# An HGRN2 attention and PReLU network kernel on one core: f, q and v loaded one step further ahead

## The chip, the cores and the metric

The kernel runs on one core of one Trainium2 chip. The metric is the device time of one execution in microseconds (us); smaller is better. A time is the median of the runs shown. One execution is also recorded by the hardware profiler, and its trace is what the text reads.

## The reference

Two blocks stand one behind the other. The first is a gated linear recurrence for 4 batches, 8 heads, 768 positions and a head dimension of 48; the second is a two-layer network with 3072 rows, 384 inputs and 2048 hidden units.

```python
f = 1.0 / (1.0 + np.exp(-f_logit))
state = np.zeros((B, H, D, D)); y = np.zeros_like(q)
for t in range(S):
    state = f[:, :, t, :, None] * state + np.einsum('bhd,bhe->bhde', k[:, :, t], v[:, :, t])
    y[:, :, t] = np.einsum('bhd,bhde->bhe', q[:, :, t], state)

x = y.transpose(0, 2, 1, 3).reshape(B * S, H * D)        # 3072 x 384
h = x @ w_in                                              # 384 x 2048
g = np.maximum(h, 0.0) + alpha * np.minimum(h, 0.0)
out = g @ w_out                                           # 2048 x 384
```

## The kernel before

The work is cut into twelve steps. A step takes 128 positions of two batches; the steps alternate between the two pairs of batches (`bp` 0 and 1), so that steps n and n+2 belong to the same pair. For each step three parts are defined: `preparation` (the gates' running products, on VectorE, ScalarE and GpSimd), `attention` (the scores, the output products and the state) and `network` (the two layers, the second one with seven products per 2x2 blocks instead of eight, named A to E).

Nothing schedules this on its own. Each part stores its pieces of work under short words, and one list, `ORDER`, names word and step in the order in which they are issued; each engine runs its share of that list strictly in turn. `ORDER` is made by `flat` from two tables: `FIRST`, written out word for word for the opening, and `USUAL`, which is repeated for n = 4 to 12. In `USUAL` a word without a mark belongs to step n, `-` to step n-1, `+` to step n+1. So one block n issues attention of step n, most of the network of step n-1 and the preparation of step n+1. A word whose step is 12 or more is dropped.

The words that matter here:

- `ld` loads a step's inputs in five DMAs: `ld.0` is f, `ld.1` is q, `ld.2` is k (512 KB each, L343), `ld.3` and `ld.4` are the two halves of v (192 KB each, L348). For steps above 4 they are issued by SyncE (SP). In `USUAL` they stand in the first line, behind the score products `r0`, `x0`, `r1`, `x1` of step n, and load step n+1.
- f, q and k have one buffer each (`mine`, one buffer per tag). f is read last in a preparation by `le` (a product on VectorE, L235 `ut<-ut,f`), q by `qc` (a copy on ScalarE, L354). k is read by the score products `r0` and `r1` of its own step, and thus by the next block; its load has to wait for them.
- v lies in `vs`, one tile for each pair of batches, which also holds the state in other rows. v of step n is read by the state products `pd` (L655) and the output products `y0`, `y1` (L730) of block n.
- `mv` (L767) moves the attention's output `y` into the network's input `xT` with ten small DMAs, four issued by SP, four by ScalarE, two by GpSimd. The first layer of that step, `n0` to `n7` (L799), reads it in the next block.
- `km` (L492) moves the transposed keys `kt` into `ksn` with sixteen small DMAs, all from SP. `ksn` shares its buffer with `y`, so the first of them waits until all of `xT` has landed. `pd` of the next block reads `ksn`.
- `d1` and `e` end with the two stores of a step's output (L845), also from SP.

Each DMA issued by SP or ScalarE takes the next of eight completion counters in turn, and is issued only once the DMA that had that counter before, eight such DMAs earlier, has landed.

```python
def loads():
    return {"A": nc.scalar, "G": nc.gpsimd, "V": nc.sync}.get(letter[0], nc.gpsimd if 0 < n <= FROM else nc.sync)
...
several(w, "ld" + mark, [lambda a=a: load(*a) for a in (("f", fT), ("q", qT), ("k", kT))]
        + [lambda cc=cc: load_v(cc) for cc in range(NC2)])
```

Of the kernel before, what the change touches and what calls it, by code (L numbers as in the profile page):

```python
# [67 lines left out]
"""  # L68

USUAL = """  # L70
r0 R0 x0 X0 n0- g0- G0- n1- g1- G1- r1 R1 x1 X1 n2- g2- G2- n3- g3- G3- S0- pd of oc0 oc1 m0 n4- g4- G4- ld+ sg+ kr+ qc+ l1+ l2+ l3+ c0+ c1+ c2+
c3+ n5- g5- G5- n6- g6- G6- n7- g7- G7- S1- sc+ A1- B- ka- le+ k4+ e2+ p00A p01A p02A p03A p10A p11A p12A p13A y0 y1 C1- D- u2- ke+ kt+ e3+ e4+ sa+
e5+ m1 z0A z1A mv A2- C2- d0- oa- e6+ km+ e7+ sb+ fs+ E- u3- b- d1- s00+ s01+ s10+ s11+ e-
"""

STEPS = 12
FROM = 4


def flat(first, usual):  # L80
    out = []
    for token in first.split():
        word, step = token.split(":")
        out.append((word, int(step)))
    for n in range(FROM, STEPS + 1):
        for token in usual.split():
            step = n + {"+": 1, "-": -1}.get(token[-1], 0)
            if step < STEPS:
                out.append((token.rstrip("+-"), step))
    return out  # L90


ORDER = flat(FIRST, USUAL)


# [935 lines left out]
```

## Time and profile before

| | before |
|---|---|
| median of 3 runs | 607.54 us (607.3 to 616.0) |
| profiled execution | 607.44 us, span 605.6 us |
| TensorE (PE) busy | 585.1 us, 97% of the span |
| VectorE (DVE) busy | 489.6 us, 81% |
| ScalarE (ACT) busy | 242.4 us, 40% |
| GpSimd (POOL) busy | 102.9 us, 17% |
| mean DMA rate | 83 GB/s, 50.41 MB |

The page gives each engine's busy time and its share of the span; a table of 40 slices shows where in the span it falls, and the chain of waits follows the work that ended last back through what released it. The "timeline" lists instructions with their start, their duration and, in brackets, the idle time before them. For a DMA the time shown is that of its issue on the engine's queue (SPq is SP's, ACTq is ScalarE's); when its data has landed is told separately, as the time from issue to landing. The span is 1.84 us shorter than the profiled execution's own time.

In the usual blocks the steps repeat every 47 us. The xT moves of steps 4 to 11 are issued at 222, 269, 316, 363, 411, 458, 505 and 552 us of the span.

### The profile page before, as it was taken

The page shows a single profiled execution, that of the slowest core. Times are in us where ns is not written, and L with a number is a line of the kernel's source. Part 1 is how long each engine was busy: PE and PEld are TensorE (multiplying, and loading weights), DVE is VectorE, ACT ScalarE, POOL GpSimd, SP SyncE. Part 2 cuts the span into 40 slices and gives each one's busy share as a digit, 9 for nine tenths or more (in the row PEclk, how much of TensorE's full clock was granted, in tenths as well). Part 3 has the DMA queues.
Part 4 walks back from the last instruction along what each step waited for, and adds up shares of the span by engine and source line. Part 5 has one row for each costly group of instructions (what it writes and reads, how often), then busy time and mean ns, then how long its engine had stood idle before and what let it go on. Part 6 is the DMA issues. An engine that isn't in the chain of part 4 may idle for free.

```text
span 605.6 us, 18807 instructions
## 1 busy us (share of the span) xinstructions
PE 585.1 (97%) x8042; PEld 527.7 (87%) x8042; DVE 489.6 (81%) x990; ACT 242.4 (40%) x464; POOL 102.9 (17%) x142
## 2 busy tenths in 40 slices
PE   3799999999999999999999999999999999999998
PEld 2699767898998899899899899799899899889997
DVE  8898999896868889889889899889899889761251
ACT  5688824433311542452452361271261362223110
POOL 6538562654230000000000000000000000000000
PEclk9999999999999999999999999999999999999999
DMA  8786272222112513402502502502602601201000
GB/s 286 241 298 225 72 258 52 65 59 45 49 35 29 162 27 58 130 22 37 155 11 42 160 3 50 162 0 45 169 0 42 166 8 39 44 2 28 27 0 27
DMA packets 73955, 50.41 MB, mean 83 GB/s; under 512 B 47264, under 2 KB 63264, under 8 KB 73872
## 3 DMA queue, kind: packets, MB, share of 16 engines
q1 hardware_dynamic: 65616, 39.07, 23.8%
q10 hardware_dynamic: 7216, 8.30, 4.7%
q0 software_dynamic: 1040, 1.84, 1.2%
q8 instruction: 64, 1.05, 0.7%
q14 instruction: 19, 0.16, 0.1%
HBM read 36.21 MB, written 4.72 MB: 68 GB/s over the span
## 4 chain that ended last, share of the span: by engine, by line
PE 92%; DMA 3%; DVE 2%; ACT 1%; issue 1%; SPq 0%; DVEq 0%
PE ph L799 37%; PE pa L894 10%; PE pc L894 9%; PE pd L894 5%; PE pb L894 5%; PE pe L894 5%; PE py L730 4%; PE ph L817 4%; PE qu L537 3%; PE raw L517 3%; PE po L859 3%; DMA w_in_raw<-in_w_in 2%; PE state L655 2%; PE off L617 1%; DMA k<-in_kT 1%
## 5 line engine op out<-in xcount | busy, mean ns | idle before, releaser
L799 PE MATMUL ph<-xT,w_in_sb 128*128 128x256 f32 x1056 | 237.2, 382 | 0.9 <-DVE gate L809 0.6
L799 PEld LDWEIGHTS ph<-xT,w_in_sb 128*128 128x128 f32 x1056 | 198.0, 190 | 30.9 <-issue 1.7
L809 DVE SCALAR_TENSOR_TENSOR gate<-neg,om,ph 128x256 f32<-128x256 f32 x176 | 76.3, 476 | 48.8 <-ACT neg L805 48.5
L805 ACT ACTIVATE neg<-ph 128x512 f32<-128x512 f32 x88 | 51.7, 598 | 156.5 <-PE ph L799 134.6
L767 POOL DMA_DIRECT2D xT<-y x22 | 12.0, 549 | 373.6 <-ACT y L739 371.2
L894 PE MATMUL pa<-w_out_sb,gate 128*128 128x192 f32 x352 | 61.9, 328 | 0.0
L894 PE MATMUL pc<-t,S 128*128 128x192 f32 x352 | 61.6, 328 | 0.0
L894 PEld LDWEIGHTS pa<-w_out_sb,gate 128*128 128x128 f32 x352 | 57.8, 190 | 1.9 <-DVE gate L809 1.0
L894 PEld LDWEIGHTS pc<-t,S 128*128 128x128 f32 x352 | 57.4, 190 | 0.6
L544 DVE COPY_PREDICATED ad<-mquad,qu 128x160 f32<-128x160 int32 (+6 forms) x140 | 41.5, 299 | 5.5
L524 DVE COPY_PREDICATED ad<-mraw,raw 128x256 f32<-128x256 int32 (+2 forms) x96 | 41.1, 444 | 4.7 <-ACT ad L582 2.0
L235 DVE TENSOR_TENSOR ut<-ut,fs 128x128 f32<-128x128 f32 (+7 forms) x62 | 41.0, 663 | 0.8
L453 ACT COPY A<-q 48x512 f32<-48x512 f32 x40 | 24.7, 617 | 38.4 <-DVE q L235 38.0
L368 ACT COPY ut<-qd 128x256 f32<-128x256 f32 (+1 forms) x52 | 32.0, 633 | 12.1 <-DVE qd L235 10.0
L920 ACT ACTIVATE o<-pa 128x192 f32<-128x192 f32 x11 | 3.6, 331 | 69.1 <-PE pa L894 65.4
L898 DVE SCALAR_TENSOR_TENSOR Csum<-pc,Csum 128x192 f32<-128x192 f32 x22 | 7.9, 358 | 28.6 <-PE pc L894 28.3
L894 PE MATMUL pd<-w_out_sb,S 128*128 128x192 f32 x176 | 30.5, 326 | 0.2 <-DVE gate L809 0.2
L894 PE MATMUL pb<-t,gate 128*128 128x192 f32 x176 | 30.5, 327 | 0.0
L716 ACT COPY A<-ad 32x256 f32<-32x256 f32 x74 | 29.6, 400 | 2.1 <-DVE ad L544 0.7
L894 PE MATMUL pe<-w_out_sb,S 128*128 128x192 f32 x176 | 30.4, 326 | 0.0
L894 PEld LDWEIGHTS pd<-w_out_sb,S 128*128 128x128 f32 x176 | 28.8, 190 | 0.4 <-ACT neg L805 0.4
L894 PEld LDWEIGHTS pb<-t,gate 128*128 128x128 f32 x176 | 28.9, 190 | 0.1
(137 smaller groups left out, 837.0 us busy)
## 6 DMA issues: line engine op xcount, KB each, us to landing
w_in_raw<-in_w_in SPq DMA_DIRECT2D x7, 767.2 KB, 7.7
f<-in_fT SPq DMA_DIRECT2D x10, 512.0 KB, 4.2
q<-in_qT SPq DMA_DIRECT2D x10, 512.0 KB, 5.1
out<-o SPq DMA_DIRECT2D x23, 192.0 KB, 2.1
w_out_raw<-in_w_out SPq DMA_DIRECT2D x5, 767.8 KB, 7.3
k<-in_kT SPq DMA_DIRECT2D x7, 512.0 KB, 7.2
vs<-in_v SPq DMA_DIRECT2D x16, 192.0 KB, 7.2
ksn<-kt SPq DMA_DIRECT2D x80, 32.0 KB, 2.0
```

Source lines behind the costliest of these rows:

```text
L235: (nc.gpsimd if beside[0] else nc.vector).tensor_tensor(*a)
L368: w[f"c{r}{mark}"] = lambda r=r: nc.scalar.copy(q4()[:, gs, :, r], qdv[r][:, gs, :, 0])
L453: copy(A[halves(cc)[1], u0:u1, par * HP:(par + 1) * HP, CH * cc:CH * (cc + 1)], x["q3"][rows(par)].rearrange("p (u h c) s t -> p u h c (s ...
L524: nc.vector.copy_predicated(adu[:, :, :, d:4], mraw[:, d, :, d:4].bitcast(I32).unsqueeze(1).broadcast_to((128, H, NB, n_)), rv[:, :, QO[d] ...
L544: nc.vector.copy_predicated(ad[:, u, :, :, 4 * m:DB], mquad[:, lo:lo + n_].bitcast(I32).unsqueeze(1).unsqueeze(1).broadcast_to((128, 2, HP ...
L716: copy(A[s_, u, :, s_], ad[s_, u].rearrange("p r h t -> p (r h) t"))
L730: nc.tensor.matmul(to[64 * par:64 * par + 64, u, o:o + CH], lhsT=vs[bp][:, cc, u, hd * D:hd * D + 64], rhs=A[:, u, par * HP + hp, CH * cc: ...
L799: nc.tensor.matmul(ph[f][:, j * T:(j + 1) * T], lhsT=w_in_sb[:, kt, m * 128:(m + 1) * 128], rhs=x["T"][:, kt], start=(kt == 0 and j == 0), ...
L805: nc.scalar.activation(neg[f], ph[f].rearrange("p (j t) -> p j t", j=2), AF.Relu, scale=-1.0)
L809: nc.vector.scalar_tensor_tensor(gate[:, m % NH, m // NH], neg[f][:, j], om[:, m:m + 1], ph[f].rearrange("p (j t) -> p j t", j=2)[:, j], A ...
L817: nc.tensor.matmul(ph[u, g][:, j * C:(j + 1) * C], lhsT=w_in_sb[:, kt, m * 128:(m + 1) * 128], rhs=x["T"][:, kt, u * C:(u + 1) * C], start ...
L894: nc.tensor.matmul(p[name][:, 0:DH], lhsT=of(f), rhs=by(f), start=(f == 0 and not more), stop=(f == NH - 1), skip_group_check=True)
```

## The change

Only the order is changed, in the table `USUAL` and in `flat`, which reads it. `ld+` becomes `ld.2+`: of step n+1 only k is loaded at the old place. The loads of f, q and both halves of v go behind `mv`, with a second `+`: they belong to step n+2. For n = 4 the loads of step 5 that no earlier block has issued are put ahead of k at the old place. No instruction is added or taken away.

```diff
-... m0 n4- g4- G4- ld+ sg+ kr+ qc+ l1+ l2+ l3+ c0+ c1+ c2+
+... m0 n4- g4- G4- ld.2+ sg+ kr+ qc+ l1+ l2+ l3+ c0+ c1+ c2+
-e5+ m1 z0A z1A mv A2- C2- d0- oa- e6+ km+ e7+ sb+ fs+ E- u3- b- d1- s00+ s01+ s10+ s11+ e-
+e5+ m1 z0A z1A mv ld.0++ ld.1++ ld.3++ ld.4++ A2- C2- d0- oa- e6+ km+ e7+ sb+ fs+ E- u3- b- d1- s00+ s01+ s10+ s11+ e-
@@ def flat
-            step = n + {"+": 1, "-": -1}.get(token[-1], 0)
+            step = n + token.count("+") - token.count("-")
+            if token == "ld.2+" and n == FROM:
+                out += [(word.rstrip("+"), step) for word in usual.split() if word.endswith("++")]
```

The order moves on SP alone; the other four engines issue the same instructions in the same order. In the middle of the program SP issues before, from the xT moves of step 7 (`xT_3_4380`) on, with the loads of step 9 (`f_4_4742` and what follows) at the end of the stretch:

```order
98 L767 DMACopy xT_3_4380<-y_3_4377 48x2x128
99 L767 DMACopy xT_3_4380<-y_3_4377 16x2x128
100 L767 DMACopy xT_3_4380<-y_3_4377 48x2x128 x2
101 L492 DMACopy ksn_4_4411<-kt_4_4367 32x8x32 x4
102 L492 DMACopy ksn_4_4411<-kt_4_4367 32x8x16 x4
103 L492 DMACopy ksn_4_4411<-kt_4_4367 32x8x32 x4
104 L492 DMACopy ksn_4_4411<-kt_4_4367 32x8x16 x4
105 L845 DMACopy out<-o_0_3_4446 128x384
106 L845 DMACopy out<-o_0_3_4407 128x384
107 L343 DMACopy f_4_4742<-in_fT 128x2x512
108 L343 DMACopy q_4_4744<-in_qT 128x2x512
109 L343 DMACopy k_4_4746<-in_kT 128x2x512
```

The same stretch of SP's order in the changed kernel (its lines of code stand two lower, and the numbers at the ends of the names are counters):

```order
98 L769 DMACopy xT_3_4380<-y_3_4377 48x2x128
99 L769 DMACopy xT_3_4380<-y_3_4377 16x2x128
100 L769 DMACopy xT_3_4380<-y_3_4377 48x2x128 x2
101 L345 DMACopy f_4_4391<-in_fT 128x2x512
102 L345 DMACopy q_4_4393<-in_qT 128x2x512
103 L350 DMACopy vs_76<-in_v 64x2x384 x2
104 L494 DMACopy ksn_4_4417<-kt_4_4367 32x8x32 x4
105 L494 DMACopy ksn_4_4417<-kt_4_4367 32x8x16 x4
106 L494 DMACopy ksn_4_4417<-kt_4_4367 32x8x32 x4
107 L494 DMACopy ksn_4_4417<-kt_4_4367 32x8x16 x4
108 L847 DMACopy out<-o_0_3_4452 128x384
109 L847 DMACopy out<-o_0_3_4413 128x384
```

f, q and v of step 9 now stand ahead of the sixteen ksn moves and the two stores instead of behind them; the ksn moves have four large loads between themselves and the xT moves. This happens in six blocks, n = 4 to 9.

At the first block of the usual table (n = 4) the five loads of step 5 keep their place, but k goes from the third to the last of them. SP's order there, before:

```order
55 L343 DMACopy f_2_2638<-in_fT 128x2x512
56 L343 DMACopy q_2_2640<-in_qT 128x2x512
57 L343 DMACopy k_2_2642<-in_kT 128x2x512
58 L348 DMACopy vs_76<-in_v 64x2x384 x2
59 L767 DMACopy xT_2_2802<-y_2_2799 48x2x128
60 L767 DMACopy xT_2_2802<-y_2_2799 16x2x128
61 L767 DMACopy xT_2_2802<-y_2_2799 48x2x128 x2
62 L492 DMACopy ksn_2_2833<-kt_2_2789 32x8x32 x4
```

And SP's order at that place in the changed kernel:

```order
55 L345 DMACopy f_2_2638<-in_fT 128x2x512
56 L345 DMACopy q_2_2640<-in_qT 128x2x512
57 L350 DMACopy vs_76<-in_v 64x2x384 x2
58 L345 DMACopy k_2_2644<-in_kT 128x2x512
59 L769 DMACopy xT_2_2802<-y_2_2799 48x2x128
60 L769 DMACopy xT_2_2802<-y_2_2799 16x2x128
61 L769 DMACopy xT_2_2802<-y_2_2799 48x2x128 x2
62 L345 DMACopy f_3_2813<-in_fT 128x2x512
63 L345 DMACopy q_3_2815<-in_qT 128x2x512
64 L350 DMACopy vs_75<-in_v 64x2x384 x2
```

Here v overtakes k, and the first of the six moved groups, f, q and v of step 6, follows the xT moves of step 4.

More of the change, by code (lines that the diff above doesn't have):

```diff
@@ L70 @@
 USUAL = """
-r0 R0 x0 X0 n0- g0- G0- n1- g1- G1- r1 R1 x1 X1 n2- g2- G2- n3- g3- G3- S0- pd of oc0 oc1 m0 n4- g4- G4- ld+ sg+ kr+ qc+ l1+ l2+ l3+ c0+ c1+ c2+
+r0 R0 x0 X0 n0- g0- G0- n1- g1- G1- r1 R1 x1 X1 n2- g2- G2- n3- g3- G3- S0- pd of oc0 oc1 m0 n4- g4- G4- ld.2+ sg+ kr+ qc+ l1+ l2+ l3+ c0+ c1+ c2+
 c3+ n5- g5- G5- n6- g6- G6- n7- g7- G7- S1- sc+ A1- B- ka- le+ k4+ e2+ p00A p01A p02A p03A p10A p11A p12A p13A y0 y1 C1- D- u2- ke+ kt+ e3+ e4+ sa+
-e5+ m1 z0A z1A mv A2- C2- d0- oa- e6+ km+ e7+ sb+ fs+ E- u3- b- d1- s00+ s01+ s10+ s11+ e-
+e5+ m1 z0A z1A mv ld.0++ ld.1++ ld.3++ ld.4++ A2- C2- d0- oa- e6+ km+ e7+ sb+ fs+ E- u3- b- d1- s00+ s01+ s10+ s11+ e-
 """
```

## The prediction

> **What bounds the kernel now.** I read the page first, then PE's waits from 187 us of the span on, where the usual blocks begin, then busy time by stretch, and last the timeline of one block. The page names the bound: PE.
>
> ```profile
> span 605.6 us, 18807 instructions
> PE 585.1 (97%) x8042; PEld 527.7 (87%) x8042; DVE 489.6 (81%) x990; ACT 242.4 (40%) x464; POOL 102.9 (17%) x142
> PE 92%; DMA 3%; DVE 2%; ACT 1%; issue 1%; SPq 0%; DVEq 0%
> ```
>
> 97% is an average over the span; what counts is the part that the change touches. PE's waits after 187 us are a single row, and the stretches show where it lies (columns: window, its length, then PE busy, weight loads, DVE, ACT, POOL, granted clock, DMA share, GB/s):
>
> ```profile
> PE off L617 <- issue: 0.9, 1, 0.9
> 0.00:187.00 187.00, 170.44 (x2586) 149.07 (x2586) 161.92 (x314) 97.31 (x185) 94.22 (x126) 1.00 0.45 137
> 187.00:223.00 36.00, 36.00 (x591) 31.88 (x590) 30.87 (x64) 15.50 (x30) 0.62 (x2) 1.00 0.32 79
> 364.00:412.00 48.00, 47.07 (x658) 42.81 (x657) 41.71 (x85) 18.37 (x35) 0.98 (x3) 1.00 0.27 67
> 412.00:459.00 47.00, 47.00 (x658) 42.82 (x658) 41.59 (x86) 18.43 (x35) 1.20 (x3) 1.00 0.28 69
> ```
>
> PE is busy 36.00 us of 36 and 47.00 of 47; only the stretch from 364 has a gap, 48.00 - 47.07 = 0.93 us, and its releaser is "issue", which means no engine and no load. Of PE's idle 605.6 - 585.1 = 20.5 us, 187 - 170.44 = 16.6 us lie in the opening, which the change leaves alone, and the last 3 us behind PE's last product. So a move of loads can gain 0.9 us at most as long as PE's own work stays, and can cost whatever it makes PE wait.
>
> **Who needs what, and when.** One block as the timeline has it, from the output products of step 9 on (start, duration, engine):
>
> ```profile
> 454.57 2.15 PE L730 MATMUL py<-A,vs 128*64 128x64 f32 x64
> 455.68 1.20 DVE L235 TENSOR_TENSOR ut<-ut,f 128x1024 f32<-128x1024 f32 x1
> 457.87 3.14 SPq L767 DMA_DIRECT2D xT<-y  x4
> 457.87 2.56 ACTq L767 DMA_DIRECT2D xT<-y  x4
> 461.83 1.25 DVE L485 STREAM_TRANSPOSE kt<-ks 128x1024 f32<-128x1024 f32 x1
> 463.15 11.99 SPq L492 DMA_DIRECT2D ksn<-kt  x16
> 471.53 5.45 PE L799 MATMUL ph<-xT,w_in_sb 128*128 128x256 f32 x24
> 475.25 1.01 SPq L845 DMA_DIRECT2D out<-o  x2
> 476.31 0.44 SPq L343 DMA_DIRECT2D f<-in_fT  x1
> 476.80 0.49 SPq L343 DMA_DIRECT2D q<-in_qT  x1
> 476.91 0.92 PE L517 MATMUL raw<-qd,k 48*32 48x80 f32 x64
> 477.86 0.37 SPq L343 DMA_DIRECT2D k<-in_kT  x1
> 478.27 1.32 SPq L348 DMA_DIRECT2D vs<-in_v  x2
> 483.98 0.94 PE L655 MATMUL state<-vs,ksn 64*48 64x48 f32 x64
> 489.10 1.06 ACT L352 ACTIVATE f<-f 128x1024 f32<-128x1024 f32 x1
> 503.65 1.22 DVE L235 TENSOR_TENSOR k<-k,kr 128x1024 f32<-128x1024 f32 x1
> ```
>
> The DMA part of the page has the sizes and the median time from issue to landing over all blocks:
>
> ```profile
> f<-in_fT SPq DMA_DIRECT2D x10, 512.0 KB, 4.2
> q<-in_qT SPq DMA_DIRECT2D x10, 512.0 KB, 5.1
> k<-in_kT SPq DMA_DIRECT2D x7, 512.0 KB, 7.2
> vs<-in_v SPq DMA_DIRECT2D x16, 192.0 KB, 7.2
> xT<-y SPq DMA_DIRECT2D x33, 48.0 KB, 2.2
> ```
>
> **Part 1, the wait that goes: none.** f lands at 476.31 + 4.2 = 480.5 us and is read first at 489.10: 8.6 us early. q lands at 481.9 and is read behind f; v is read no earlier than the output products, a block after those at 454.57; k lands at 485.1 and is read at 503.65. Nothing waits for these loads today, so loading them earlier is worth 0 us.
>
> **Part 2, can they start there?** f's buffer is free when the product at 455.68 ends, 456.9 us; v's when the output products end, 456.7. SP's four xT issues end at 461.0. So no load waits for its buffer (the nearest margin is 461.0 - 456.9 = 4.1 us), and nothing behind them on SP is held up by that. They take SP 0.44 + 0.49 + 1.32 = 2.25 us, until 463.3. The first ksn move was issued at 463.15, because kt ends at 461.83 + 1.25 = 463.1. On SP itself the loads thus fit into a pause: 0.1 us late.
>
> **Part 3, what is queued behind them: the sixteen ksn moves, two stores, k.** The first four moves use counters of older DMAs; moves five to eight wait for f, q and the two halves of v to land, by the turn of the counters; the last eight wait for the first eight. When does v land? In the block shown v's landing times are
>
> ```profile
> DMA to landing us min/median/max: 7.9/8.0/8.1
> ```
>
> so its second half, issued at about 479.0, lands at 487.0, and five loads of 3 x 512 + 2 x 192 = 1920 KB take 487.0 - 476.31 = 10.7 us. f, q and v are 1408 KB: 10.7 x 1408 / 1920 = 7.8 us, from 461.0 to 468.8. Upper bound: the whole 10.7 us, 471.7. The eighth ksn move then goes at about 468.8, and eight more at 11.99 / 16 = 0.75 us each end at 474.8. Before, the sixteen ended at 463.15 + 11.99 = 475.1. I take 475.5, since the moves were partly waiting for each other anyway. The landing times of ksn in that block:
>
> ```profile
> DMA to landing us min/median/max: 1.9/2.0/3.8
> ```
>
> The last one lands at 477.5 (479.3 with the longest), and the state products read ksn at 483.98. **Cover: 4.7 to 6.5 us** per block. Cost 0; were the cover gone, PE would stand still for the difference in each of six blocks.
>
> As the k row shows beside f's (7.2 against 4.2 us, with f and q queued ahead of it), a DMA lands later behind others of its queue. [...]
>
> The xT moves stand ahead of the loads on SP, and ScalarE's are issued by 457.87 + 2.56 = 460.4. With 2.2 us they land by 463.2; the first layer reads xT at 471.53, 8.3 us later. Cost 0.
>
> The two stores follow at 475.5 + and end within half a us of before. k waits for the score products that end at 476.91 + 0.92 = 477.8 in both kernels, then has the DMA engines to itself. In block 4 alone k goes behind v; with 18 us to spare (503.65 - 485.1) this is 0.
>
> **Part 4, the one gap.** How the loads lie beside PE's work changes (columns as above, in the block shown):
>
> ```profile
> 461.00:470.00 9.00, 9.00 (x71) 8.78 (x78) 8.79 (x16) 0.37 (x2) 0.00 (x0) 1.00 0.25 37
> 476.30:482.00 5.70, 5.70 (x148) 4.79 (x147) 4.30 (x12) 1.05 (x2) 0.00 (x0) 1.00 0.96 296
> ```
>
> During the loads the DMA engines are 96% busy, and PE goes through 148 matmuls in 5.7 us; where f, q and v will lie it goes through 71 in 9 us, and the DMA engines are 25% busy. The gap of 0.93 us came while loads were under way (SP and PE, two blocks earlier; the last row is from the page's list of DMA queues: packets, MB, share):
>
> ```profile
> 380.59 0.44 SPq L343 DMA_DIRECT2D f<-in_fT  x1
> 383.41 1.33 SPq L348 DMA_DIRECT2D vs<-in_v  x2
> 389.98 0.74 PE L617 MATMUL off<-q,kh 48*32 48x32 f32 x62
> 391.65 0.24 PE L617 MATMUL off<-q,kh 48*32 48x32 f32 x2 [0.93 <-issue]
> q8 instruction: 64, 1.05, 0.7%
> ```
>
> PE stopped inside a row of like products, waiting for no engine; I read it as instructions that had not arrived, since the list has a DMA queue that moves instructions and the DMA engines were taken. That happened in one of seven such windows. Bounds: -0.93 us if this goes with the loads' place, 0 if it is chance, +0.93 if a new one comes. I take -0.5, the middle between gone and kept, because the busiest mixture of loads and short products goes. [...]
>
> **The sum.** The profiled execution took 607.44 us (span 605.6 and 1.84 around it), 0.1 below the median of 607.54. 607.44 + 0 (waits) + 0 (queue) - 0.5 = **606.9 us**.
>
> **The rivals.**
>
> *Moves behind the loads (slower).* All sixteen ksn moves are held until the last load has landed, with xT drawn in by sharing DMA engines. At the upper bound that is 471.7; sixteen moves then end at 483.7 and land at 485.7 to 487.5, so that the state products stand still 1.7 to 3.5 us, six times: 10 to 21 us, 617.6 to 628.4. It decides from the point where ksn lands over 6.5 us later than I have it. For it: the k row, and a DMA share of 0.96 under loads. Against it: v alone at 468.8 and only four of the sixteen tied to loads; even all sixteen behind 468.8 would end at 480.8 and land at 482.8, still 1.2 us in time. Chance 0.07; between the two ends it crosses 2% (619.7), so 0.04 of it is beyond.
>
> *The gap goes wholly, and nothing else.* 607.44 - 0.93 = 606.5. It is inside my range; chance 0.35, beside 0.53 for the forecast itself with the gap half certain or kept (606.9 to 607.5).
>
> *The loads do not get ahead.* If a buffer were free later than I read it, say f's only after SP has reached its load, all of ksn would shift by that wait. It needs more than 4.1 us of delay to begin and 4.7 more to reach PE; what it gives short of that is 607.4 again. Chance 0.02.
>
> *A new wait elsewhere* (more gaps of the 0.93 kind, one in each of the six blocks, in the score products that run while k is loaded): 607.44 + 5.6 = 613.0. Chance 0.03; against it stands that k alone is 512 of the 1920 KB.
>
> **How the numbers follow.** Faster by over 2% would be below 595.4, and the blocks hold 0.93 us of idle PE: 0.01 for what I don't see. Slower by over 2% needs the first rival's upper part: 0.04. Within 2%, which is about what a measurement of this kernel can tell from no change: 0.95. The range: 606.5 with some 0.5 for the runs' scatter below, hence 605.9; above, two gaps of the 0.93 kind on top of 607.5 give 609.4. That leaves out the first rival, the last one and the tails, less than 2 in 10.
>
> **What would show it.** In the changed profile the loads of f, q and v stand at about 461 us of this block (SP's queue), the sixteen ksn moves still end near 475 to 476, and no row "PE state L655 <- DMA ksn" or "PE ph L799 <- DMA xT" appears among PE's waits. Each usual block stays at 47.0 us. ksn's longest landing time rises from 3.8 to about 6 us, as its first moves stand behind v. I am wrong if the state products wait for ksn, if SP shows a wait of the f load on DVE, or if PE's "issue" gaps after 187 us grow beyond 2 us.

## The result and the profile after

| | before | after |
|---|---|---|
| median of 22 runs each, in turn on one chip | 610.22 us (607.0 to 616.0) | 607.21 us (605.54 to 609.36) |
| ratio, 95% interval | | 0.9956 [0.9938, 0.9974] |
| profiled execution, span | 607.44 us, 605.6 | 608.01 us, 606.2 |

The changed kernel is faster by 0.44%, by the ratio 2.7 us of 610 with an interval of 1.6 to 3.8 (the medians lie 3.0 us apart). That lies within 2%, at 607.21 us where 606.9 was forecast; but the forecast gain was 0.5 us. The two profiled executions even stand the other way round, so the gain has to be read from the stretches and not from the spans. The head of the page after, with the chain:

```profile
span 606.2 us, 18821 instructions
PE 585.0 (97%) x8042; PEld 527.6 (87%) x8042; DVE 489.8 (81%) x990; ACT 242.1 (40%) x464; POOL 102.4 (17%) x142
PE 81%; DVE 2%; ACT 1%; issue 1%; DVEq 0%
```

PE is the bound as before. Busy time by stretch, with the columns of the prediction:

```profile
0.00:187.00 187.00, 168.77 (x2575) 147.48 (x2576) 160.50 (x311) 97.01 (x185) 93.79 (x126) 0.97 0.45 137
364.00:411.00 47.00, 47.00 (x658) 42.82 (x658) 41.72 (x86) 18.53 (x36) 1.07 (x2) 1.00 0.28 69
462.00:470.00 8.00, 8.00 (x51) 8.00 (x50) 7.82 (x14) 0.33 (x1) 0.00 (x0) 1.00 0.86 217
476.00:482.00 6.00, 6.00 (x149) 5.06 (x148) 4.62 (x13) 0.60 (x1) 0.00 (x0) 1.00 0.49 155
```

The opening, which both kernels share, was slower in this execution (168.77 us of PE work in 187, against 170.44). The stretch from 364 us, where the one gap was, is full: 47.00 of 47.00. PE has no wait left after 187 us, neither for an engine nor for "issue". The DMA engines are now 86% busy at 462 to 470 us, beside 51 long matmuls, and 49% at 476 to 482, beside 149 short ones. SP's queue and the state products of the same block:

```profile
458.52 3.10 SPq L769 DMA_DIRECT2D xT<-y  x4
461.73 0.57 SPq L345 DMA_DIRECT2D f<-in_fT  x1
462.91 1.39 SPq L350 DMA_DIRECT2D vs<-in_v  x2
464.53 12.25 SPq L494 DMA_DIRECT2D ksn<-kt  x16
478.52 0.39 SPq L345 DMA_DIRECT2D k<-in_kT  x1
484.63 0.94 PE L657 MATMUL state<-vs,ksn 64*48 64x48 f32 x64
```

The ksn moves end at 476.8 us, 18.3 us behind the start of the xT moves (before: 475.14 - 457.87 = 17.3): 1.0 us later, with the state products still 7.9 us away.

### The profile page after: what moved, and what is told of

It reads as the page before. It is cut to its first block, busy times and chain, and to the rows that moved or that the text cites. A ratio compares the mean times of both kernels' runs of the same rounds, so it can differ in the third digit from the quotient of the medians.

```text
span 606.2 us, 18821 instructions
## 1 busy us (share of the span) xinstructions
PE 585.0 (97%) x8042; PEld 527.6 (87%) x8042; DVE 489.8 (81%) x990; ACT 242.1 (40%) x464; POOL 102.4 (17%) x142
## 4 chain that ended last, share of the span: by engine, by line
PE 81%; DVE 2%; ACT 1%; issue 1%; DVEq 0%
PE ph L801 37%; PE pa L896 10%; PE pc L896 9%; PE pd L896 5%; PE pb L896 5%; PE pe L896 5%; PE py L732 3%; PE qu L539 3%; PE raw L519 2%; PE state L657 1%; PE off L619 1%; DVE ad L546 1%; DVE w_out_sb L237 0%; ACT A L455 0%; DVE gate L811 0%
## 5 line engine op out<-in xcount | busy, mean ns | idle before, releaser
L519 PE MATMUL raw<-qd,k 48*32 48x80 f32 x1536 | 22.6, 243 | 6.8 <-DVE qd L237 6.8
```

The lines of the kernel that those rows point to most:

```text
L519: nc.tensor.matmul(to[DB * j:DB * (j + 1), par, hp * C:hp * C + QW], lhsT=x["k"][r_, g * DB:(g + 1) * DB], rhs=qd[r_, g], start=True, stop ...
```

## The experiments

There are three theories. A *gap* is a time in which PE stands still and the profile names nothing that it waited for ("issue"); the *burst* is the loads of f, q, k and v that go out together, 1920 KB in the kernel before. **Collision**: the instructions of PE come late while a burst of loads is under way beside short products, and the change takes most of the burst away from there. **Lead**: f, q or v is sometimes late in executions that were not profiled. **Opening**: the gain lies outside the usual blocks or is scatter.

For every profile I read two things: the gaps of PE after 187 us, and how long the seven usual blocks take, from SP's first xT move of step 4 to that of step 11. All of them together, in the order in which they are explained below:

```
profile                              xT(4)    xT(11)   blocks   gaps of PE, us
before                               222.11   551.65   329.54   0.93
before, 2nd                          223.08   553.82   330.74   1.05  0.90
before, 3rd                          221.23   551.07   329.84   1.21
before, 4th                          221.97   554.21   332.24   1.88
before, 5th                          222.33   557.86   335.53   1.76  1.82
after                                224.01   552.30   328.29   none
after, 2nd                           221.02   549.34   328.32   none
after, 3rd                           223.36   551.46   328.10   none
no f, q, v                           223.81   552.19   328.38   none
after, two loads added behind k      221.14   553.14   332.00   1.89
f, q, v behind the ksn moves         222.32   552.55   330.23   0.95  0.24
before, 28 small matmuls added       223.39   553.69   330.30   1.72
after, 28 small matmuls added        226.83   555.15   328.32   none
before, two loads added              222.22   556.50   334.28   3.68
```

**The kernel before, against itself.**

> The kernel before, unchanged, against itself. Every theory: ratio 1.000 within the interval. What the second profile tells: the theory of collision (PE's instructions come late while the burst of loads is under way beside short products) expects one to five gaps of about 0.9 us after 187 us of the span, released by issue, all inside the 11 us behind a load of f; the theory of lead (f, q or v sometimes lands too late in the unprofiled slow executions) expects waits of ACT or PE on a DMA of f, q or vs there; the theory of the opening (the gain lies before the usual blocks, or is scatter) expects the usual blocks free of gaps and the opening to vary by 2 us or more.

Ratio 0.9974 [0.9945, 1.0004]: a comparison can be off by a quarter of a per cent. The gaps in its timeline (start, duration, engine, and in brackets the idle time ahead):

```profile
392.54 0.24 PE L617 MATMUL off<-q,kh 48*32 48x32 f32 x2 [1.05 <-issue]
440.45 0.45 PE L617 MATMUL off<-q,kh 48*32 48x32 f32 x29 [0.90 <-issue]
```

The first stands at the very instruction at which the first profile had its only gap: behind 62 of the 64 products of off. A gap by chance would hardly come back there. The second is one block later, 29 products before the end. Counted in the trace, PE's instructions behind the two gaps are number 11457 and 12737 (from 0 on, weight loads included): five times 256 apart. No wait on a DMA of f, q or vs was seen.

**No loads of f, q and v.** From step 6 on they are left out, and the steps compute on what the buffers hold; k is loaded as before.

```diff
+            if token == "ld+" and step > FROM + 1:
+                token = "ld.5+"                       # only k; f and q keep the tiles of step 5
```

> Leaves out the loads of f, q and v of steps 6 to 11 (they compute on what is there), k and all else as before. The theory of collision: 1408 of 1920 KB are gone from the burst, so the gaps go and the time comes to that of the changed kernel, ratio 0.993 to 0.997, no issue gap after 187 us. The theory of lead: nothing can be late any more, the same ratio. The theory of the opening: ratio 1.000, as the opening is the same.

0.9964 [0.9945, 0.9983], no gap, 328.38 us for the blocks: without the burst of f, q and v the gaps are gone. This takes away lateness too, so it does not part collision from lead.

**The burst put back, the lead kept.** The changed kernel with two loads into `kt` and `k4`, which are dead at that point.

```diff
-... G4- ld.2+ sg+ ...
+... G4- ld.2+ xl sg+ ...        # xl: kt <- fT, k4 <- qT, 512 KB each, on SP
```

> The changed kernel, with two loads of 512 KB added behind k in the blocks 4 to 10, into buffers that nobody reads before they are written anew: f, q and v keep their lead, but the burst beside the short products is 1536 KB again (before: 1920). The theory of collision: gaps released by issue come back, about 0.9 us each, one or more in the profile, and the ratio goes back to 0.998 to 1.005. The theory of lead: f, q and v are as early as in the changed kernel, ratio 0.993 to 0.997. The theory of the opening: 0.996 or 1.000, no gap in the usual blocks.

0.9990 [0.9965, 1.0016], and one gap, at the same instruction, 11457:

```profile
391.35 0.25 PE L626 MATMUL off<-q,kh 48*32 48x32 f32 x2 [1.89 <-issue]
```

f, q and v were as early as in the changed kernel, and the blocks take 332.00 us again. The lead theory does not explain this; the collision theory does.

**f, q and v behind the ksn moves**, at nearly the old time.

```diff
-... mv ld.0++ ld.1++ ld.3++ ld.4++ A2- C2- d0- oa- e6+ km+ e7+ ...
+... mv A2- C2- d0- oa- e6+ km+ ld.0++ ld.1++ ld.3++ ld.4++ e7+ ...
```

> The changed kernel with f, q and v of step n+2 behind the sixteen ksn moves instead of ahead of them: they go about 1 us earlier than in the kernel before (ahead of the two stores), beside the same short products. The theory of collision: as before, ratio 0.998 to 1.002, issue gaps in the profile. The theory of lead: 1 us of lead out of 8.6 is nothing, also 1.000. The theory of the opening, if it is k's new place behind v at step 5: 0.996, since that is kept here.

0.9982 [0.9962, 1.0002]; its interval holds 1.000 and comes near the changed kernel's 0.9956, so the time alone decides nothing. The profile does: a gap of 0.95 us at instruction 11457 again, and a small one of 0.24 us in front of 7361, sixteen times 256 earlier. Both stand there with k's new place behind v kept, which the opening theory had as a possible cause of the gain.

**The changed kernel again.**

> The changed kernel once more. The theory of collision: no gap released by issue after 187 us in a second profile, and a ratio of 0.995 to 0.999 (one to two gaps of 0.9 to 1.0 us gone, 1 to 2 us of 608, with the scatter of the opening on top). The theory of scatter (the first ratio of 0.9956 was mostly the opening's luck, as the unchanged kernel got 0.9974 against itself): 0.998 to 1.002.

0.9972 [0.9953, 0.9992], no gap. The gain is there a second time, smaller: 1.7 us of 608.5. The ratio alone would not prove it, since the kernel before against itself gave 0.9974.

**The boundaries moved.** 28 small matmuls in the opening, before and after the change; their results are overwritten.

```diff
-... c0b:0 iq.24:0 zm:0 ...
+... c0b:0 iq.24:0 ig:0 zm:0 ...          # ig: 28 matmuls of 128x128 by 128x32
```

> The kernel before with 28 small matmuls (56 PE instructions) added where PE idles in the opening; their results are overwritten. In the two profiles of the kernel before, all gaps released by issue after 187 us stand at places 256 PE instructions apart by a whole number (PE instruction 11457 and 12737, both 193 over a multiple of 256). The theory of collision with the fetch of instructions: the boundaries come 56 instructions earlier in the program, so that one falls into block 7, behind 62 of the 64 pairs of off, at about 345 us, and a gap of 0.9 to 2 us appears there, which no profile had; the one of the next block falls into the middle of off (behind about 34 pairs), where a smaller gap may stand, and none stands behind 62 pairs any more. Any theory in which the place in the program counts, and not the count of instructions: the gap stays behind 62 pairs of off of block 8, at about 392 us. The time: ratio 0.999 to 1.003.

> The changed kernel with the same 28 small matmuls. The theory of collision: no gap behind the instruction boundaries anywhere after 187 us, wherever they fall, since only k's 512 KB lie beside the short products; the ratio as the changed kernel's, 0.995 to 0.999. A theory by which the changed kernel was only lucky with the place of its boundaries: a gap of 0.9 us in block 7 or 8, ratio 0.998 to 1.002.

The kernel before: 1.0028 [1.0005, 1.0051], with its only gap at another place of the program:

```profile
299.81 0.25 PE L617 MATMUL off<-q,kh 48*32 48x32 f32 x4 [1.72 <-issue]
```

The gap behind off of the old block, 392 us, is gone; a new one stands two blocks earlier, in front of instruction 8897, which is again 193 over a multiple of 256. My expectation had named the block between (345 us), since I had counted 56 added instructions. The trace shows each of these matmuls as two products with two weight loads (x8098 matmuls on the page, 8042 before), so 112 were added, and in the kernel before the boundary (8897) stands 108 instructions behind the 62nd product of off in just that block at 297 us. So 112 more instructions put the boundary four instructions, or two products, ahead of that place, and the gap stands four products before the end instead of two. The count decides where the gap is, not the place in the program.

The changed kernel with the same shift has no gap at any boundary after 187 us (one of 1.27 us ends at 152.48 us, in the opening, in front of instruction 4801, also 193 over a multiple of 256) and 328.32 us for the blocks. Its ratio, 1.0005 [0.9985, 1.0025], missed what I expected. Its profile has a longer opening (226.83 us until xT of step 4, against 221 to 224 in the others), which may be the reason; that is not shown. Against the shifted kernel before it is 607.9 / 609.72 = 0.997, without an interval.

**A larger burst.**

```diff
-... G4- ld+ sg+ ...
+... G4- ld+ xl sg+ ...
```

> The kernel before with two more loads of 512 KB behind its five (into buffers that nobody reads before they are written anew): 2944 KB in one burst beside the short products, which lasts until about 491 us instead of 487 of the block shown. The theory of collision: more and longer gaps than the 0.9 and 1.9 us in all of the two profiles of the kernel before: 2 to 6 us, at the same instruction boundaries, ratio 1.000 to 1.010. The theory of lead and the theory of the opening: f, q, k and v land as before, 1.000.

1.0056 [1.0030, 1.0083], and a longer gap at instruction 11457, but only one:

```profile
394.54 0.25 PE L624 MATMUL off<-q,kh 48*32 48x32 f32 x2 [3.68 <-issue]
```

**How the fetch stands to the gap.** By now nine profiles have the burst beside short products, and each has a gap; five have at most the 512 KB of k there, and none of these has a gap after 187 us. All twelve gaps stand in front of an instruction that is 193 over a multiple of 256. The DMA records of the trace hold 64 packets of 16384 bytes on the queue marked instruction (q8); 64 x 256 = 16384 is close to PE's 16345 instructions, so by an estimate from these two counts one packet holds 256 of them. The table has the packet that ends last before PE goes on at instruction 11457, and when PE passed the boundary before that one, instruction 11201, in us of each span:

```
kernel                    11201   packet starts  ends     product ahead   product behind   behind - end
before                    388.59  389.45         390.38   390.52          391.65           1.27
before, 2nd               389.36  390.26         391.13   391.30          392.53           1.40
before, 3rd               387.71  388.33         389.70   389.65          391.05           1.35
before, 4th               388.69  390.12         391.19   390.39          392.46           1.27
before, 5th               388.60  389.97         391.24   390.54          392.49           1.25
two loads behind k        387.34  389.04         389.99   389.28          391.35           1.36
f, q, v behind ksn        389.14  389.94         390.88   391.08          392.22           1.34
before, two loads         388.73  392.05         393.14   390.67          394.54           1.40
after                     390.36  389.72         390.82   392.28          392.28           1.46
after, 2nd                387.46  386.47         387.60   389.38          389.38           1.78
after, 3rd                389.55  388.65         389.66   391.47          391.47           1.81
no f, q, v                390.26  389.33         390.39   392.18          392.18           1.79
```

In the eight profiles with a gap here PE went on 1.25 to 1.40 us behind the end of the packet; at the four gaps in front of other boundaries it was 1.34 to 1.46 us. Without the burst the packet ended 1.46 to 1.81 us ahead of need, and PE did not stand still. With the burst the packet starts late: 0.6 to 3.3 us behind PE's passing of instruction 11201, where without it it starts 0.6 to 1.0 us ahead. The packet itself took 0.9 to 1.4 us with a gap and 1.0 to 1.1 us without, so a slower packet is the smaller part. From its start until PE went on 2.2 to 2.7 us passed, while PE, not held up, goes from 11201 to 11457 in 1.9 us. So by an estimate from these rows a packet has to start 0.3 to 0.8 us before PE passes the boundary ahead of it. Beside long products there is more room: 64 state products take 0.94 us, 48 of the first layer 10.63 us.

By these rows a packet that starts late is the mechanism, and its margin without a burst is only some tenths of a us at this boundary: in the first profile of the changed kernel the 1.46 us are as few as behind the smallest gap, and with the added matmuls instruction 8897 followed 1.36 us behind its packet, just without a gap. That such a gap can never come in the changed kernel is not shown. What holds the packet's start back, the DMA engines or something ahead of them, the runs do not show.

**More profiles of both, for the size.**

> The kernel before, a third profile, to size the term: how long the seven usual blocks take from the xT moves of step 4 to those of step 11. So far 329.5 and 330.7 us with one and two gaps, against 328.3 us in all four kernels without the burst beside the short products. The theory of collision: at least the gap behind PE instruction 11457, 329 to 332 us. If the whole first difference of 2.7 us came from the usual blocks, the mean of the profiles of before must come near 331.0; if part of it was the opening, it stays near 330.

> The kernel before, a fourth profile, for the same count: 329 to 332 us and one to three gaps by the theory of collision.

> The kernel before, a fifth profile, for the same count: 329 to 332 us and one to three gaps by the theory of collision.

> The changed kernel, a third profile: 328.3 us from the xT moves of step 4 to those of step 11 and no gap released by issue after 223 us, by the theory of collision; a gap in one of three profiles would say that the change makes the gaps rarer and does not end them.

The five profiles of before have 329.54 to 335.53 us, mean 331.6; the three of after 328.10 to 328.32, mean 328.2. The difference of 3.3 us lies in the interval of the first measured gain (2.7 us, 1.6 to 3.8) and above that of the second (1.7 us, 0.5 to 2.9), and the mean of before is over the 331.0 that I had set: the usual blocks alone account for the gain. Five profiles are few, and one of them carries nearly half of it; the fourth and the fifth lie over the 332 us that I had expected at most.

That one, the fifth, has gaps of 3.58 us in all, but its blocks took 335.53 - 328.2 = 7.3 us more. Its PE after the first gap, beside the same products of the changed kernel (the second fence), and its stretches:

```profile
392.49 0.24 PE L617 MATMUL off<-q,kh 48*32 48x32 f32 x2 [1.76 <-issue]
392.66 12.31 PE L799 MATMUL ph<-xT,w_in_sb 128*128 128x256 f32 x48
...
392.00:396.00 4.00, 3.51 (x10) 2.85 (x11) 3.50 (x6) 1.26 (x4) 0.00 (x0) 0.61 0.01 4
396.00:400.00 4.00, 4.00 (x19) 3.47 (x19) 1.51 (x3) 2.65 (x4) 0.00 (x0) 0.97 0.00 0
392.90:396.20 3.30, 3.30 (x9) 2.59 (x9) 2.60 (x4) 1.13 (x4) 0.00 (x0) 0.50 0.02 5
```

```profile
392.44 10.63 PE L801 MATMUL ph<-xT,w_in_sb 128*128 128x256 f32 x48
```

The 48 products take 12.31 us instead of 10.63, and the granted clock, the third number from the end, is 0.61 for the 4 us around the end of the gap and 0.50 in the 3.3 us of the last row. The trace's clock records have this half clock for 3.41 us, from 392.84 on. This gap is paid a second time: 1.76 idle and 1.68 of slower products. The lower clock came again behind its second gap (0.76 and 0.82 in the two windows of 4 us from 442 us on), and in the fourth profile behind its one gap (0.59 in the 4 us from 392 us on). So of the mean difference of 3.3 us the gaps themselves are 1.9 (9.55 us in five profiles) and the half clock about 1.0 (three times 1.7 in five profiles); the other 0.4 us has no cause that the runs show.

## Why the prediction was right, and where its size was not

**What bounds the kernel: right.** PE is busy without a break in the usual blocks of the changed kernel, and no computing engine waits for f, q, k or v. What SP waits for before it issues a load (5.1 us in all for the score products ahead of k, and 1.1 us once for an xT move ahead of f) never reaches PE.

**Part 1 to 3, waits and queue at nothing: right.** In the block shown the loads went out at 461.73 us without a wait for their buffers. The ksn moves ended 1.0 us late, not 0.4; their longest landing time rose from 3.8 to 4.3 us in the block shown and to 5.2 in others, where about 6 was forecast. Two things make the difference: the loads took about 7 us and not 7.8 (in the block from 364 us the second half of v was issued at 369.33 and landed 5.3 us later, 7.1 us behind the issue of f at 367.48), and the first ksn move went out 2.8 us behind the f load and not 2.15. The cover of 4.7 to 6.5 us held. The moves did land behind the loads, as forecast: in that block v's second half landed at 374.62 and the first four ksn moves at 374.84 to 375.35. PE paid nothing for it.

**Part 4, the one gap: the mechanism right, the size wrong.** "Bounds: -0.93 us if this goes ... I take -0.5" is the term that was sized wrong, and with it "can gain 0.9 us at most". It was read from one execution, which was a good one: among five profiles of before its blocks are the shortest. The term measures 3.3 us by the profiles, and 2.7 or 1.7 by the times. Two things were left out. The gap is no chance event of one window in seven: it hangs on where the boundaries of 256 instructions fall. In the kernel before it came at instruction 11457 in five of five profiles, where only its length varied (0.93 to 1.88 us), and at 12737 in two of five. And the five gaps of 1.76 us or more were each followed by a lower clock (0.57 to 0.82 in windows of 4 us laid on it), which at 1.76 us about doubled the price (1.68 us of slower products). The full -0.93 of the rival "the gap goes wholly" was the right event, at too low a price. That PE's instructions had not arrived was the author's reading of the one gap; the runs have since shown all twelve gaps at such boundaries (in front of 7361, 8897, 11457 and 12737, all 193 over a multiple of 256), where they cost 0.24 to 3.68 us, and at the other boundaries after 187 us no gap.

**The median.** The sum started from 607.44 us, "0.1 below the median". That median was of three runs; over 22 it was 610.22. The forecast of 606.9 lies near 607.21 by luck: the base was low by 2.8 us, the gain by 2.5 (3.0 by the medians instead of 0.5), and the two errors nearly cancel.

**The rivals.** Moves behind the loads: no row shows the state products waiting. Loads that do not get ahead, and new gaps in the score products beside k: neither was seen.

**Left open.** How large the gain is: the first ratio was 0.9956, the second 0.9972, and before against itself gave 0.9974, so the first may hold some luck. That the gaps go is shown by the profiles; what this is worth in the median is known only within the two intervals, 0.5 to 3.8 us. What delays the start of the packets is open too.

## What to carry to other kernels

A wait put down to "issue" inside a row of like products is worth counting: in this kernel the instructions behind all twelve such gaps differed by multiples of 256, and a packet of the instruction queue had ended 1.25 to 1.46 us before PE went on. The cure here was to move large transfers beside long products that use few instructions (51 matmuls in 8 us, against 149 in 6), and not to make the data earlier. Rank the places of a load by how many instructions the bound engine goes through during the transfer, and not only by who waits for the data. And a term read from a single execution needs a second profile before its value is taken as a bound.

## What the hardware showed that was not expected

PE went on 1.25 to 1.40 us behind the end of a 16 KB packet of the instruction queue, in eight of eight gaps at instruction 11457. After 187 us, gaps of 0.24 to 1.21 us left the granted clock alone, and so did one of 1.72 us (clock 1.000 over that whole execution); those of 1.76, 1.82, 1.88, 1.89 and 3.68 us were each followed by a stretch of lower clock, which by the windows of 4 us cost 1.68 to 1.72 us (in the fifth profile of the kernel before 0.50 from 392.90 to 396.20 us, 3.41 us long by the trace's clock records). The length of the gap alone does not decide: in the opening of the changed kernel a gap of 1.16 us, which ended at 60.34 us, was followed by the half clock (0.50 from 60.60 to 63.90 us), and in that of the kernel before a gap of 1.45 us, which ended at 70.60 us, was not (1.00 from 70.70 to 74.10 us). What else decides, these few gaps do not show.
